# A state-space convolution block: the input's first transform by whole-array matmuls

## The chip, the cores and the metric

The kernel runs on one core of a Trainium2 chip. The metric is the device time of one execution in microseconds (us). A core has a matmul engine (TensorE, PE in the profile), a vector engine (VectorE, DVE), a scalar engine (ScalarE, ACT) that computes functions, a general engine (GpSimd, POOL) and a sync engine (SyncE, SP) that here only issues transfers. TensorE writes to PSUM; VectorE or ScalarE takes the results out ("evacuates" them) to SBUF. Transfers between SBUF and main memory run on 16 DMA engines shared by all queues.

## The reference

The block normalizes its input, runs a long convolution over the sequence, adds the result back through a gate, and then runs a gated feed-forward network. `L` is 2048, `D` is 640. Cut to what matters here:

```python
K = einsum("dn,dnl,dn->dl", Cc, exp(dt*A*l), dt*Bc).real
h = layernorm(x) * (1 + ca) + sa                 # sa, ca, ga, ... = silu(c) @ w_mod
y = irfft(rfft(pad(h)) * rfft(pad(K)))[:L] + h * Dskip
x = x + ga * y
h = layernorm(x) * (1 + cb) + sb
x = x + gb * ((silu(h @ w1) * (h @ w3)) @ w2)
```

The convolution is done per column of `D` over the 2048 positions.

## The kernel before, in words

A position is written as l = 64 a + b, with a below `NA` = 32 and b below `NB` = 64. The transform has two stages: one over a for each b, giving 32 complex frequencies f, and one over b for each f. The host lays the input out with b outermost, so a tile of 128 rows (`ln1_load`, line 366) holds four values of b, each with its 32 values of a. There are 16 such tiles.

The scale (1 + ca) is moved out of the transform into the gate. What is left of the modulation is to add the row r = sa / (1 + ca) to every normalized position. Since the transform is linear, this adds the column sums of the transform's matrix times r. `mod_shift` (line 313) prepares this as `rrow` (r on 64 partitions, line 325) and as `shift` (the product, 320 columns wide with the halves of `D` on the two halves of the partitions, lines 326 to 335).

`u_stage1` (line 389) transforms one tile. For each of its four b it multiplies a 32 by 64 matrix (`s1r`, real and imaginary parts side by side) with 32 rows of the tile, separately for the two halves of `D`: eight matmuls, each on its own 32x64 piece of the array, since the two halves of `D` go to the two halves of the partitions. Two PSUM areas take the results: Z for the first two b, A or B, by the parity of the tile, for the others. In even tiles four matmuls with one row each first put the shift into Z, so that ScalarE can evacuate it with a plain copy (line 409). All other evacuations are VectorE additions of `shift` (lines 411 and 412). Then one transfer stores the tile (line 413) to the scratch `us` in main memory, laid out as half of `D`, part, f, b, columns. A and B are used by the exponentials too (`exp_fast`, `exp_slow`).

`u_load` (line 549) reads it back for the second stage: the convolution's columns are taken in five blocks of 128, and a step fetches eight frequencies of a block to the tile `uk`, with the real part on partitions 0 to 63 and the imaginary part on the others, b within them. It takes two transfers, and four in the third block, which lies across the two halves of `D`. `stage2` (line 559) multiplies input and convolution kernel of a block.

Beside this the kernel makes the convolution kernel: `phases` on GpSimd, sines and exponentials on ScalarE, table products on VectorE (lines 497 to 508), `kgen` and `k_stage1` on TensorE. A first loop over `tk` (10 steps) starts this up. In its first six steps it calls `u_stage1` for two tiles each; tiles 0 to 3 come before it. In it also run `polar` for the remaining columns and `mod_cols`, which multiplies projection weights; the weights are fetched on the same sync queue as the stores and loads of the scratch. At step 7 the loads of the first block are issued. After the loop follow rounds in an order written out by hand (`ROUND`).

ScalarE's instructions stay in the order of the program (`act`, `acopy`). In the loop before the rounds, most instructions of TensorE and VectorE may be reordered by the compiler, which plans with its own cost estimates; at run time each engine's order is fixed.

Of the kernel before, what the change touches and what calls it, by code (L numbers as in the profile page):

```python
# [9 lines left out]
F32 = mybir.dt.float32  # L10
# [3 lines left out]
OP = mybir.AluOpType  # L14
# [3 lines left out]
P = 128  # L18
L = 2048
D = 640  # L20
F = 1728
NA, NB = 32, 64
DC = 128
# [6 lines left out]
KD = D // P  # L30
NFT = 14
WC = 384
# [5 lines left out]
def consts():  # L38

    a = np.arange(NA)[:, None]  # L40
    f1 = np.arange(NA)[None, :]
    ang = 2 * np.pi * a * (f1 + 0.25) / NA
    s1 = np.zeros((4, NA, 2, 4, NA))
    s1r = np.zeros((4, NA, 2, NA))
    for q in range(4):
        s1[q, :, 0, q, :] = np.cos(ang)
        s1[q, :, 1, q, :] = -np.sin(ang)
        s1r[q, :, 0] = np.cos(ang)
        s1r[q, :, 1] = -np.sin(ang)
    s1 = s1.reshape(P, 2, P)  # L50
    s1r = s1r.reshape(P, 2 * NA)
    b = np.arange(NB)[:, None, None]
    g1 = np.arange(NA)[None, :, None]
    f2 = np.arange(NB)[None, None, :]
    th = 2 * np.pi * (b * (g1 + 0.25) / L + b * f2 / NB)
    s2 = np.zeros((2, NB, NA, 2, NB))
    s2[0, :, :, 0] = np.cos(th)
    s2[1, :, :, 0] = np.sin(th)
    s2[0, :, :, 1] = -np.sin(th)
    s2[1, :, :, 1] = np.cos(th)  # L60
    s2 = s2.reshape(P, NA, P)

    i1 = (s2.transpose(2, 1, 0) / L).reshape(2, NB, NA // 2, 2, P).transpose(3, 1, 2, 0, 4).reshape(P, NA // 2, 2, P)
    i2 = np.concatenate([np.cos(ang).T, -np.sin(ang).T] * 2)

    iota = np.zeros((P, NPH), np.int32)
    iota[:, :NA] = -(128 * np.arange(NA) + 63)
    iota[:, NA:] = 2 * np.arange(NA) + 1

    selx = np.tile(np.eye(NA), (4, 1))  # L70
    stepx = np.concatenate([np.arange(NB), 64 * np.arange(NA)])[None].repeat(P, 0)

    c1 = s1r.reshape(4, NA, 2 * NA).sum(axis=1, keepdims=True).repeat(NA, axis=1).reshape(P, 2 * NA)

    one4 = (np.arange(P) % NA == 0).astype(np.float32)[:, None]

    toq = np.arange(P)[:, None] % 4 == np.arange(P)[None] // NA
    tog = np.arange(P)[:, None] // 4 == np.arange(NA)[None]
    misc = np.concatenate([selx, stepx, s1r, c1, one4, toq, tog], axis=1)
# [28 lines left out]
def tile_kernel(ctx: ExitStack, tc: tile.TileContext, a):  # L108
    nc = tc.nc
    V, S, G, PE = nc.vector, nc.scalar, nc.gpsimd, nc.tensor  # L110

    dram = ctx.enter_context(tc.tile_pool(name="dram", bufs=1, space=DRAM))
    us = dram.tile([2, 2, NA, NB, D // 2], F32, name="us")
    zs = dram.tile([NDC, NB, 2, NA, DC], F32, name="zs")
    xs = dram.tile([NT, P, D], F32, name="xs")

# [1 line left out]
    ident = cp.tile([P, P], F32, name="ident")  # L118
# [18 lines left out]
    def acopy(out, in_):  # L137
        return tc.keep_in_program_order(S.copy(out, in_))  # L138
# [15 lines left out]
    s1 = kp.tile([P, 2, P], F32, name="s1")  # L154
# [28 lines left out]
    rrow = pm_.tile([P, D], F32, name="rrow")  # L183
    shift = pm_.tile([P, D // 2], F32, name="shift")
    cols = pm_.tile([P, 7, KD], F32, name="cols")
    lt = pm_.tile([P, 2, D - DC], F32, name="lt")
    misc = pm_.tile([P, 9 * NA + 1 + P], F32, name="misc")
    selx, stepx = misc[:, :NA], misc[:, NA:4 * NA]
    s1r, c1, one4 = misc[:, 4 * NA:6 * NA], misc[:, 6 * NA:8 * NA], misc[:, 8 * NA:8 * NA + 1]
    toq, tog = misc[:, 8 * NA + 1:8 * NA + 1 + P], misc[:, 8 * NA + 1 + P:]  # L190
    tiny = pm_.tile([P, 1], F32, name="tiny")
    V.memset(tiny, -1e-35)

# [119 lines left out]
    def mod_shift():  # L313

        sa, ca, ga, zero, inv, r, gs = (cols[:, i] for i in range(7))
        V.tensor_scalar(ca, ca, 1.0, None, op0=OP.add)
        V.tensor_scalar(zero, ca, 0.0, 1e-18, op0=OP.is_equal, op1=OP.mult)
        V.tensor_tensor(ca, ca, zero, op=OP.add)
        V.reciprocal(inv, ca)
        V.tensor_tensor(r, inv, sa, op=OP.mult)  # L320

        pr = psS.tile([P, 2, 512], F32, name="pr", tag="Z", bufs=1).rearrange("p a b -> p (a b)")
        for k in range(KD):
            PE.matmul(pr[:64, k * P:(k + 1) * P], r[:, k:k + 1].broadcast_to([P, 64]), ident, start=True, stop=True)
        V.tensor_copy(rrow[:64], pr[:64, :D])
        rc = pm_.tile([P, WC], F32, name="part", bufs=2)[:, :KD * 2 * NA].rearrange("p (k c) -> p k c", k=KD)
        V.tensor_tensor(rc, bc(c1, 1, KD), bc(r, 2, 2 * NA), op=OP.mult)
        ps = psS.tile([P, 512], F32, name="ps", tag="pk", bufs=1)
        for k in range(KD):
            for hh in range(2):  # L330
                lo, hi = max(k * P, hh * 320), min(k * P + P, hh * 320 + 320)
                if lo < hi:
                    PE.matmul(ps[hh * 64:hh * 64 + 64, lo - hh * 320:hi - hh * 320], rc[:, k],
                              ident[:, lo - k * P:hi - k * P], start=True, stop=True, tile_position=(0, hh * 64))
        V.tensor_copy(shift, ps[:, :320])

    def mod_gate():

# [24 lines left out]
    hpz = pre.enter_context(tc.tile_pool(name="hpz", bufs=2, side="right"))  # L363
# [19 lines left out]
            x = xt[2 * p + i]  # L383
            act(x, x, AF.Identity, scale=rs[:, 1, i:i + 1], bias=rs[:, 2, i:i + 1])

    usw = us.rearrange("h c f b d -> (h c f) b d")
    usr = us.rearrange("h c f b d -> h c b f d")

    def u_stage1(j):


        x = xt[j]
        u = hpz.tile([P, 4, D // 2], F32, name="u", bufs=2)
        pu = [psS.tile([P, 2, 512], F32, name="pu", tag=t, bufs=1) for t in ("Z", "AB"[j % 2])]
        one = j % 2 == 0
        for q in range(2 if one else 0):
            for hh in range(2):
                PE.matmul(pu[0][hh * 64:hh * 64 + 64, q, :320], c1[q * NA:q * NA + 1],
                          rrow[q * NA:q * NA + 1, hh * 320:hh * 320 + 320],
                          start=True, stop=False, tile_position=(q * NA, hh * 64))  # L400
        for h in range(2):
            for q in range(2):
                r0 = (2 * h + q) * NA
                r = slice(r0, r0 + NA)
                for hh in range(2):
                    PE.matmul(pu[h][hh * 64:hh * 64 + 64, q, :320], s1r[r], x[r, hh * 320:hh * 320 + 320],
                              start=not (one and h == 0), stop=True, tile_position=(r0, hh * 64))
        if one:
            acopy(u[:, :2, :], pu[0][:, :, :320])
        else:  # L410
            V.tensor_tensor(u[:, :2, :], pu[0][:, :, :320], bc(shift, 1, 2), op=OP.add)
        V.tensor_tensor(u[:, 2:, :], pu[1][:, :, :320], bc(shift, 1, 2), op=OP.add)
        nc.sync.dma_start(usw[:, 4 * j:4 * j + 4, :], u)


    ph, cs, AA, EC, PK, K1 = {}, {}, {}, {}, {}, {}
# [132 lines left out]
    def u_load(ch, i):  # L549

        fs = slice(i * 8, i * 8 + 8)
        for h in range(2):
            lo, hi = max(ch * DC, h * 320), min(ch * DC + DC, h * 320 + 320)
            if lo < hi:
                for c in range(2):
                    nc.sync.dma_start(uk[c * 64:c * 64 + 64, 0, fs, lo - ch * DC:hi - ch * DC],
                                      usr[h, c, :, fs, lo - h * 320:hi - h * 320])

    def stage2(ch, g):
        s2 = fp.tile([P, 4, P], F32, name="s2", bufs=3)  # L560
# [207 lines left out]
    rest = polar(d1, G)  # L768
# [5 lines left out]
    for tk in range(LAG):  # L774
# [46 lines left out]
        if tk == 7:  # L821
            for i in range(4):
                u_load(0, i)
# [60 lines left out]
    V, S, G, PE = (InOrder(tc, e, (in_order,)) for e in (V, S, G, PE))  # L884
# [544 lines left out]
```

## Time and profile before

| | us |
|---|---|
| median of 3 runs | 1014.18 |
| lowest and highest run | 1011.33, 1014.97 |
| profiled execution, its span (no other time of it is given) | 1011.9 |
| TensorE busy | 929.3 |
| VectorE busy | 729.6 |
| ScalarE busy | 541.4 |
| GpSimd busy | 347.2 |

The span runs from the first to the last instruction of the profiled execution. Busy time is given in microseconds and, on the page, as share of the span. "PEclk" is TensorE's granted clock, 1.0 being full. "DMA share" is the mean busy share of the 16 DMA engines; above 1 means that packets overlap. In a row of waits stand the waiting engine with tile and line, what it waited for, the total, the number of times and the longest. In rows of operations stand line, engine, operation, output and input tile, count, shortest, median and longest duration in ns, and the starts of the first and the last. In rows of time stand start, duration, engine, line and operation, and in brackets the idle time before it with what ended it. An f32 matmul is two MATMUL instructions, so counts of matmuls are doubled.

### The profile page before, as it was taken

How to read it: one execution, taken by the hardware profiler on the slowest of the kernel's cores; microseconds unless marked ns; L12 is line 12 of the kernel's file. 1: busy time of each engine (PE TensorE's matmuls, PEld its weight loads, DVE VectorE, ACT ScalarE, POOL GpSimd, SP SyncE). 2: the span in 40 equal slices, each digit the busy share in tenths (PEclk: the TensorE clock that was granted, in tenths of full speed). 3: DMA queues.
4: the chain of work that ended last, by engine and by line, in shares of the span. 5: the costliest groups of instructions: out<-in, count | busy, mean ns of one | idle time of the engine just before them, and what ended most of it. 6: DMA issues, size and time to landing. Idle time of an engine off the chain costs nothing.

```text
span 1011.9 us, 20628 instructions
## 1 busy us (share of the span) xinstructions
PE 929.3 (92%) x8214; PEld 691.3 (68%) x8214; DVE 729.6 (72%) x1227; ACT 541.4 (54%) x793; POOL 347.2 (34%) x330
## 2 busy tenths in 40 slices
PE   5898797998998889699999999989979999999998
PEld 2545354666666666467888888766758888888786
DVE  4588856888888885567666676688696666676765
ACT  3667665999999963256433332344643333333432
POOL 1453333444544521123322231453352222224441
PEclk9955777999999999899999999999999999999999
DMA  9463586564556687593211113879332111123352
GB/s 274 140 223 115 204 197 189 142 161 124 138 157 158 176 221 230 171 268 119 80 53 52 52 53 93 218 226 288 98 105 79 53 52 53 52 78 104 92 197 76
DMA packets 103571, 140.74 MB, mean 139 GB/s; under 512 B 20564, under 2 KB 62676, under 8 KB 103476
## 3 DMA queue, kind: packets, MB, share of 16 engines
q1 hardware_dynamic: 92692, 113.60, 39.1%
q10 hardware_dynamic: 8480, 18.09, 6.0%
q0 software_dynamic: 2304, 7.74, 2.3%
q8 instruction: 64, 1.05, 0.4%
q14 instruction: 31, 0.25, 0.1%
HBM read 107.94 MB, written 31.46 MB: 138 GB/s over the span
## 4 chain that ended last, share of the span: by engine, by line
PE 41%; DVE 5%; DMA 3%; issue 2%; ACT 1%; POOL 1%; SPq 1%; DVEq 0%; ACTq 0%; POOLq 0%
PE ps L102 41%; DMA A<-zs 3%; SPq L102 1%; DVE T L102 1%; DVE ul L102 1%; DVE xm L102 1%; DVE gl L102 1%; ACT s L102 1%; DVE s L102 1%; DMA xm<-in_x_dram 1%; ACT gh L102 0%; POOL s L102 0%; POOL S L102 0%; DVE h L102 0%; POOL rs L102 0%
## 5 line engine op out<-in xcount | busy, mean ns | idle before, releaser
L102 DVE TENSOR_TENSOR s<-ps,s 128x512 f32<-128x512 f32 x138 | 94.7, 687 | 76.8 <-PE ps L102 76.3
L472 POOL TENSOR_TENSOR ph<-thi,iota 128x1024 int32<-128x1024 int32 x40 | 85.4, 2135 | 176.1 <-DVE A L508 78.4
L102 DVE TENSOR_TENSOR gl<-rw,gh 128x640 fp32r<-128x640 f32 x87 | 88.1, 1012 | 61.4 <-ACT gh L102 60.1
L102 ACT CAST gh<-rw 128x640 fp32r<-128x640 f32 x87 | 63.2, 726 | 113.5 <-PE ps L102 80.4
L102 POOL TENSOR_TENSOR rw<-rw,gbr 128x512 f32<-128x512 f32 x56 | 81.6, 1465 | 105.4 <-DMA rw<-in_w_dram 91.7
L102 POOL TENSOR_TENSOR S<-rw 128x256 f32<-128x256 f32 x46 | 35.0, 764 | 176.2 <-DVE S0l L102 157.4
L570 PE MATMUL p<-uk,s 128*64 128x256 f32 x640 | 79.1, 390 | 13.3 <-PE pa L432 5.6
L102 PE MATMUL ps<-xA,gh 128*128 128x512 f32 x280 | 88.0, 392 | 1.1 <-DVE h L102 0.4
L102 PE MATMUL ps<-gh,uh 128*128 128x512 f32 x224 | 88.6, 396 | 0.0
L102 PE MATMUL ps<-gl,uh 128*128 128x512 f32 x224 | 88.1, 393 | 0.0
L102 PE MATMUL ps<-gh,ul 128*128 128x512 f32 x208 | 81.9, 394 | 0.0
L570 PEld LDWEIGHTS p<-uk,s 128*64 128x64 f32 x640 | 45.2, 139 | 38.6 <-PE pa L432 8.4
L102 PEld LDWEIGHTS ps<-xA,gh 128*128 128x128 f32 x280 | 52.1, 188 | 14.3 <-ACT gh L102 1.4
L102 PE MATMUL ps<-xA,gl 128*128 128x512 f32 x140 | 54.7, 391 | 1.2 <-DVE gl L102 1.2
L135 ACT ACTIVATE A<-pa 128x1024 f32<-128x1024 f32 x40 | 40.4, 1023 | 26.3 <-PE pa L432 24.9
L497 DVE TENSOR_TENSOR E<-A,cs 128x1024 f32<-128x1024 f32 x40 | 50.1, 1252 | 1.7 <-ACT A L135 1.7
L612 PE MATMUL pz<-Y,i 64*128 64x128 f32 x640 | 45.3, 286 | 5.2 <-ACT zt L138 5.0
L504 DVE TENSOR_TENSOR A<-A,ph 128x1024 f32<-128x1024 f32 x40 | 49.9, 1247 | 0.0
L612 PEld LDWEIGHTS pz<-Y,i 64*128 64x128 f32 x640 | 39.2, 191 | 15.0 <-issue 7.8
L102 PEld LDWEIGHTS ps<-gl,uh 128*128 128x128 f32 x224 | 42.8, 191 | 9.3
L102 PEld LDWEIGHTS ps<-gh,uh 128*128 128x128 f32 x224 | 42.8, 191 | 8.9
L539 PE MATMUL pt<-s,K 128*64 128x128 f32 x640 | 47.3, 291 | 0.5 <-ACT uk L138 0.5
(241 smaller groups left out, 2382.3 us busy)
## 6 DMA issues: line engine op xcount, KB each, us to landing
rw<-in_w_dram ACTq DMA_DIRECT2D x44, 320.0 KB
us<-u SPq DMA_DIRECT2D x16, 640.0 KB
s<-in_s_dram SPq DMA_DIRECT2D x40, 256.0 KB
i<-in_i_dram SPq DMA_DIRECT2D x40, 256.0 KB
rw<-in_wg_dram SPq DMA_DIRECT2D x31, 320.0 KB
rw<-in_wu_dram SPq DMA_DIRECT2D x28, 320.0 KB
uk<-us SPq DMA_DIRECT2D x32, 256.0 KB
zs<-zt SPq DMA_DIRECT2D x32, 256.0 KB
```

Source lines behind the costliest of these rows:

```text
L102: ins = fn(*args, **kw)
L135: return tc.keep_in_program_order(S.activation(*args, **kw))
L472: hold(G.tensor_tensor(p, bc(thi[:, sl], 2, NPH), bc(iota, 1, SD), op=OP.mult))
L497: keep(V.tensor_tensor(EC[s][:, :, 1:3, :], AA[s][:, :, 1:3, :], mid(cs[s]), op=OP.mult))
L504: keep(V.tensor_tensor(A[:, :, 1:3, :], A[:, :, 1:3, :], mid(ph[s]), op=OP.mult))
L539: keep(PE.matmul(pt[c * 64:c * 64 + 64, g, :], kk[:, g, :], s1[:, c, :], start=True, stop=True, tile_position=(0, c * 64)))
L570: keep(PE.matmul(p2[par * 64:par * 64 + 64, pi, c, :], s2[:, pi * 2 + par, c * 64:c * 64 + 64], uk[:, 0:kn + 1:kn, f, :], start=True, stop ...
L612: ins = keep(PE.matmul(pz[:, par, (g % 2) * 2 + pi, :], i1[r, pi, c, :], Y[r, pi, c, :], start=(c == 0), stop=(c == 1), tile_position=(par ...
```

## The change

The transform of a tile uses the matrix `s1`, 128 by 2 by 128, which holds the 32 by 32 matrix four times along its diagonal, once for the real and once for the imaginary part. It was there already, for `k_stage1`. For each of the two parts, two matmuls over all 128 rows and 128 columns, one per half of `D`, fill one PSUM area: Z for the real part, A or B for the imaginary part. Every area is evacuated by VectorE with the shift added; the one-row matmuls and ScalarE's copies are gone. `shift` becomes 2 by 640 columns on all partitions, made by two products in `mod_shift`. The scratch is laid out as part, b, f, columns; the store is still one transfer per tile, and a step of `u_load` is one transfer over 128 partitions.

```diff
-    us = dram.tile([2, 2, NA, NB, D // 2], F32, name="us")
+    us = dram.tile([2, NB, NA, D], F32, name="us")
...
+    c1 = s1.sum(axis=0).T
...
         for k in range(KD):
-            PE.matmul(pr[:64, k * P:(k + 1) * P], r[:, k:k + 1].broadcast_to([P, 64]), ident, start=True, stop=True)
-        V.tensor_copy(rrow[:64], pr[:64, :D])
-        rc = pm_.tile([P, WC], F32, name="part", bufs=2)[:, :KD * 2 * NA].rearrange("p (k c) -> p k c", k=KD)
-        V.tensor_tensor(rc, bc(c1, 1, KD), bc(r, 2, 2 * NA), op=OP.mult)
...
-        V.tensor_copy(shift, ps[:, :320])
+            PE.matmul(pr[:, k * P:(k + 1) * P], r[:, k:k + 1].broadcast_to([P, P]), ident, start=True, stop=True)
+        for c in range(2):
+            V.tensor_scalar(shift[:, c], pr[:, :D], c1[:, c:c + 1], None, op0=OP.mult)
...
-    usw = us.rearrange("h c f b d -> (h c f) b d")
-    usr = us.rearrange("h c f b d -> h c b f d")
+    usw = us.rearrange("c b f d -> (b f) c d")
+    usr = us.rearrange("c b f d -> (c b) f d")
...
         x = xt[j]
-        u = hpz.tile([P, 4, D // 2], F32, name="u", bufs=2)
...
-        if one:
-            acopy(u[:, :2, :], pu[0][:, :, :320])
-        else:
-            V.tensor_tensor(u[:, :2, :], pu[0][:, :, :320], bc(shift, 1, 2), op=OP.add)
-        V.tensor_tensor(u[:, 2:, :], pu[1][:, :, :320], bc(shift, 1, 2), op=OP.add)
-        nc.sync.dma_start(usw[:, 4 * j:4 * j + 4, :], u)
+        u = hpz.tile([P, 2, D], F32, name="u", bufs=2)
+        for c in range(2):
+            pu = psS.tile([P, 2, 512], F32, name="pu", tag="AB"[j % 2] if c else "Z", bufs=1)[:, :, :D // 2]
             for hh in range(2):
+                PE.matmul(pu[:, hh, :], s1[:, c, :], x[:, hh * 320:hh * 320 + 320], start=True, stop=True)
+            V.tensor_tensor(u[:, c].rearrange("p (h d) -> p h d", h=2), pu,
+                            shift[:, c].rearrange("p (h d) -> p h d", h=2), op=OP.add)
+        nc.sync.dma_start(usw[j * P:(j + 1) * P], u)
...
         fs = slice(i * 8, i * 8 + 8)
-        for h in range(2):
...
+        nc.sync.dma_start(uk[:, 0, fs, :], usr[:, fs, ch * DC:ch * DC + DC])
```

More of the change, by code (lines that the diff above doesn't have):

```diff
@@ L43, in consts @@
     s1 = np.zeros((4, NA, 2, 4, NA))
-    s1r = np.zeros((4, NA, 2, NA))
     for q in range(4):
@@ L47, in consts @@
         s1[q, :, 1, q, :] = -np.sin(ang)
-        s1r[q, :, 0] = np.cos(ang)
-        s1r[q, :, 1] = -np.sin(ang)
     s1 = s1.reshape(P, 2, P)
-    s1r = s1r.reshape(P, 2 * NA)
     b = np.arange(NB)[:, None, None]
@@ L71, in consts @@
     stepx = np.concatenate([np.arange(NB), 64 * np.arange(NA)])[None].repeat(P, 0)
-    c1 = s1r.reshape(4, NA, 2 * NA).sum(axis=1, keepdims=True).repeat(NA, axis=1).reshape(P, 2 * NA)
+    c1 = s1.sum(axis=0).T
     one4 = (np.arange(P) % NA == 0).astype(np.float32)[:, None]
@@ L78, in consts @@
     tog = np.arange(P)[:, None] // 4 == np.arange(NA)[None]
-    misc = np.concatenate([selx, stepx, s1r, c1, one4, toq, tog], axis=1)
+    misc = np.concatenate([selx, stepx, c1, one4, toq, tog], axis=1)
     f = lambda v: np.ascontiguousarray(v, dtype=np.float32)
@@ L182, in tile_kernel @@
     scb = pm_.tile([P, KD, NA], F32, name="scb")
-    rrow = pm_.tile([P, D], F32, name="rrow")
-    shift = pm_.tile([P, D // 2], F32, name="shift")
+    shift = pm_.tile([P, 2, D], F32, name="shift")
     cols = pm_.tile([P, 7, KD], F32, name="cols")
     lt = pm_.tile([P, 2, D - DC], F32, name="lt")
-    misc = pm_.tile([P, 9 * NA + 1 + P], F32, name="misc")
+    misc = pm_.tile([P, 5 * NA + 3 + P], F32, name="misc")
     selx, stepx = misc[:, :NA], misc[:, NA:4 * NA]
-    s1r, c1, one4 = misc[:, 4 * NA:6 * NA], misc[:, 6 * NA:8 * NA], misc[:, 8 * NA:8 * NA + 1]
-    toq, tog = misc[:, 8 * NA + 1:8 * NA + 1 + P], misc[:, 8 * NA + 1 + P:]
+    c1, one4 = misc[:, 4 * NA:4 * NA + 2], misc[:, 4 * NA + 2:4 * NA + 3]
+    toq, tog = misc[:, 4 * NA + 3:4 * NA + 3 + P], misc[:, 4 * NA + 3 + P:]
     tiny = pm_.tile([P, 1], F32, name="tiny")
@@ L323, in mod_shift @@
         for k in range(KD):
-            PE.matmul(pr[:64, k * P:(k + 1) * P], r[:, k:k + 1].broadcast_to([P, 64]), ident, start=True, stop=True)
-        V.tensor_copy(rrow[:64], pr[:64, :D])
-        rc = pm_.tile([P, WC], F32, name="part", bufs=2)[:, :KD * 2 * NA].rearrange("p (k c) -> p k c", k=KD)
[L327 to L335, printed above, removed]
+            PE.matmul(pr[:, k * P:(k + 1) * P], r[:, k:k + 1].broadcast_to([P, P]), ident, start=True, stop=True)
+        for c in range(2):
+            V.tensor_scalar(shift[:, c], pr[:, :D], c1[:, c:c + 1], None, op0=OP.mult)
     def mod_gate():
@@ L551, in u_load @@
         fs = slice(i * 8, i * 8 + 8)
[L552 to L557, printed above, removed]
+        nc.sync.dma_start(uk[:, 0, fs, :], usr[:, fs, ch * DC:ch * DC + DC])
     def stage2(ch, g):
```

12 lines of the change are left out of this document (removed).

## The prediction

> **What bounds the kernel now.** I read the page first, then a table of stretches, then the waits and the tile `pu` in the stretches that the change touches.
>
> ```profile
> span 1011.9 us, 20628 instructions
> PEclk9955777999999999899999999999999999999999
> ```
>
> Each figure of the clock row is one fortieth of the span. TensorE has half its clock around 50 to 100 us, part of it to about 175 us, and nearly all of it later. The edited code runs in that slow part. The stretches, with busy time per engine, granted clock and DMA share:
>
> ```profile
> 38.00:52.00 14.00, 11.71 (x85) 5.39 (x78) 6.33 (x16) 12.12 (x14) 9.54 (x9) 0.91 0.20 71
> 52.00:118.00 66.00, 57.97 (x696) 31.17 (x697) 56.80 (x106) 46.02 (x56) 24.87 (x24) 0.58 0.49 175
> 118.00:136.00 18.00, 14.31 (x124) 6.91 (x120) 12.36 (x19) 10.02 (x11) 8.87 (x7) 0.58 0.50 188
> 136.00:170.00 34.00, 28.77 (x405) 17.41 (x402) 20.54 (x32) 20.30 (x25) 10.95 (x6) 0.77 0.76 185
> 170.00:340.00 170.00, 154.09 (x2983) 113.10 (x2978) 147.57 (x241) 156.90 (x192) 75.31 (x47) 1.00 0.57 154
> ```
>
> Columns after the length are PE, weight loads, DVE, ACT, POOL, clock, DMA share, GB/s. From 170 us the hand-ordered rounds run against ScalarE (156.90 of 170), so what ends before 170 moves everything behind it one for one. Between 52 and 118 VectorE (56.80 of 66) and TensorE at 0.58 clock (57.97) share the bound; ScalarE has 20 us to spare. The chain of waits on the page reaches back only to 453 us, so the early part must be argued from waits:
>
> ```profile
> ACT u L138 <- PE pu L406: 9.3, 2, 7.6
> PE pu L406 <- ACT u L138: 6.2, 3, 3.6
> DVE u L412 <- PE pu L406: 5.0, 2, 4.8
> DVE u L411 <- PE pu L406: 3.3, 4, 2.0
> ```
>
> The transform and its evacuations already hold each other up: TensorE waited 6.2 us for ScalarE's copies, VectorE 8.3 us (5.0 + 3.3) for TensorE.
>
> **The change part by part.** What the transform takes now (operation rows, then the same tile by stretch):
>
> ```profile
> L406 PE MATMUL pu<-x,misc x256: 426/737/792, 41.9 to 128.2; 32*64 32x320 f32 x128
> L398 PE MATMUL pu<-rrow,misc x64: 427/736/792, 38.6 to 118.8; 1*64 1x320 f32 x64
> L412 DVE TENSOR_TENSOR u<-pu,shift x16: 805/818/826, 44.4 to 127.1; 128x640 f32<-128x640 f32 x16
> L138 ACT COPY u<-pu x8: 670/690/693, 48.7 to 126.5; 128x640 f32<-128x640 f32 x8
> ...
> 38.00:52.00 14.00, 5.64 (x36) 1.71 (x36) 0.82 (x1) 0.67 (x1) 0.91 0.20 71
> 52.00:118.00 66.00, 30.73 (x244) 9.86 (x244) 15.36 (x19) 4.11 (x6) 0.58 0.49 175
> 118.00:136.00 18.00, 4.56 (x40) 1.28 (x40) 3.24 (x4) 0.69 (x1) 0.58 0.50 188
> ...
> sum 132.00, PE 40.92 PEld 12.85 DVE 19.43 ACT 5.47; mean PE 10.23 PEld 3.21 DVE 4.86 ACT 1.37
> ```
>
> *Evacuations.* Eight copies leave ScalarE (5.47 us), eight additions of 0.82 us come to VectorE. Six of the copies lie in 52 to 118 (x6), where VectorE is idle for only 9.2 us, mostly waiting in order at its head: 6 x 0.82 = 4.9 us on the path. The bounds are 0 (all in the idle time) and 6.6 (all eight). I take 4.9. ScalarE's 5.47 us are worth nothing themselves, since it has slack; but TensorE's 6.2 us of waiting for those copies, which sat in ScalarE's written order, become waits for VectorE. I credit -2, between 0 and -6.2.
>
> *Matmuls.* Each tile of 128 rows now needs 8 matmuls on 32x64 pieces, plus 4 one-row ones for even tiles; afterwards 4 on the whole array, one behind the other. An f32 matmul shows as two passes. Prices:
>
> ```profile
> 76.86 1.35 PE L406 MATMUL pu<-x,misc 32*64 32x320 f32 x8
> 115.67 0.80 PE L406 MATMUL pu<-x,misc 32*64 32x320 f32 x16 [1.87 <-ACT u L138]
> ...
> 165.13 1.22 PE L357 MATMUL pm<-part,misc 128*128 128x256 f32 x2 [0.25 <-DVE modT L353]
> ```
>
> At half clock four pieces together took 1.35 us, at full clock eight took 0.80. As pieces run side by side, each group is two passes of 320 columns and a tail; equal tails give 2 x (1.35 - 0.80) = 1.10 us of streaming at half clock and 0.55 at full. The whole-array row agrees: 1.22 us for 256 columns at half clock is 0.88 of streaming by the same rate, and a tail of 0.34. So 16 x 4 = 64 matmuls cost 35 us at full clock and 70 at half, against 40.92 now: -6 to +29 us of TensorE time.
>
> The Trainium skill, "TensorEngine Tiling (Array Packing)", Overview and Key Properties, speaks against the edit: pieces of the array run independently, up to 16 at once. By that rule alone the old form would be 24 rounds (16 tiles and 8 one-row rounds), 26 us at half clock, and the edit would cost 44 us, an estimate. The trace bears the side-by-side running out, but not the 26 us: the old form takes 40.92, since its groups lie scattered between other shapes.
>
> Which clock? Three pieces of the slow part:
>
> ```profile
> 49.35:97.10 47.75, 45.88 (x454) 24.92 (x454) 40.01 (x72) 32.33 (x41) 20.70 (x20) 0.50 0.47 166
> 93.72:97.13 3.41, 3.41 (x80) 2.96 (x68) 2.55 (x4) 3.36 (x6) 1.59 (x2) 0.50 0.29 86
> 63.00:66.41 3.41, 3.41 (x46) 1.52 (x34) 2.13 (x6) 2.46 (x3) 1.23 (x2) 0.50 0.96 345
> 97.10:100.50 3.40, 0.15 (x2) 0.00 (x0) 3.15 (x8) 3.39 (x4) 2.35 (x2) 1.00 0.57 154
> ```
>
> TensorE shows busy 45.88 of 47.75 us and stays at 0.50. The full stretch 63.00 to 66.41, mostly 32-row pieces, did not raise the clock; the equally full 93.72 to 97.13, with 128-row operands of `kgen` and `k_stage1`, did. Then 3.4 us almost without matmuls lost it again. The new matmuls have 128 rows, so I expect rises, and losses when an evacuation keeps them waiting: about 0.75 on average. Then the 64 cost 47 us (70 x 0.5 / 0.75), 6 more than now; other TensorE work in 52 to 118, 57.97 - 30.73 = 27.2 us, falls to 21 (27.2 x 0.58 / 0.75), 6 less. Net 0 there. The Trainium skill, "TensorE: Matmul & The Clock Gate", Part 1, gives full clock after one busy window of about 3.4 us; 63.00 to 66.41 disagrees unless few rows count as idle, and 93.72 to 97.13 agrees.
>
> *Waits of VectorE.* Its 24 additions waited 8.3 us for TensorE, 0.35 each; 8 more make +2.8. Behind each stand the table products that `kgen` waits for. Bounds 0 and, at half clock where a pair of matmuls takes 2.2 us instead of 1.35, 32 x 0.85 = 27. I take 2.8, the present rate.
>
> *The first and last tiles.* Tiles 0 and 1 come at a clock of 0.91, where VectorE idles anyway:
>
> ```profile
> 44.38 0.82 DVE L412 TENSOR_TENSOR u<-pu,shift 128x640 f32<-128x640 f32 x1 [4.85 <-PE pu L406]
> 42.45 2.39 PE L406 MATMUL pu<-x,misc 32*64 32x320 f32 x18
> 41.86 0.79 PE L398 MATMUL pu<-rrow,misc 1*64 1x320 f32 x1
> ```
>
> They run from 41.86 to 44.84, 3.0 us; eight matmuls at 0.55 and a tail make 4.7: +1.7, all on the path, since the next projection matmuls queue behind. Tiles 14 and 15 (4.56 us in the 118 stretch) would take 4.7 to 9.1, with the following matmuls at the better clock: I take +1, bounds -2 and +4.5.
>
> *The shift rows.*
>
> ```profile
> 33.85 0.47 DVE L327 TENSOR_TENSOR part<-misc,cols 128x320 f32<-128x320 f32 x1
> 35.77 1.76 PE L333 MATMUL ps<-ident,part 128*64 128x128 f32 x12
> 36.02 0.82 DVE L325 COPY rrow<-pr 64x640 f32<-64x640 f32 x1 [1.05 <-PE pr L324]
> 37.57 0.49 DVE L335 COPY shift<-ps 128x320 f32<-128x320 f32 x1 [0.74 <-PE ps L333]
> ```
>
> Gone: 1.76 of TensorE and 0.47 + 0.82 + 0.49 = 1.78 of VectorE. Come: two products of 640 columns, 0.82 each by L325's row, 1.64. Bank Z is held through both, to about 37.7 instead of 36.8. I take -0.5, bounds -1.8 and +0.9.
>
> *Scratch.* Stores keep number and bytes; a partition writes two pieces instead of one. Per load step of `u_load` one DMA replaces two (four for the third channel block).
>
> ```profile
> 134.49 2.87 SPq L556 DMA_DIRECT2D uk<-us  x4
> 145.24 3.69 SPq L556 DMA_DIRECT2D uk<-us  x4
> ...
> 138.00:142.00 4.00, 0.56 1.23 199
> 4.00:5.00 1.00, 1.00 1.09 285
> ...
> 144.00:146.00 2.00, 1.00 0.30 22
> ```
>
> (After the length stand clock, DMA share and GB/s.) The sync queue issues 8 loads in 6.6 us before the rounds; four save about 3, but behind them the first `s2` loads meet busy DMA engines. The loads moved 199 GB/s with all engines busy; the parameters' 512-byte pieces, whose rows lie 2560 bytes apart, moved at 285 (4 to 5 us). The new scratch has such rows too: 2.1 MB at 285 instead of 199 is 7.4 instead of 10.5 us. No row shows the new address order, so the bounds are -3.1 and +3.1; I take -1, because the DMA engines were nearly empty from 144 to 146, so not all of a gain there reaches `p`. In the rounds (DMA share 0.57) nothing comes of it; were that cover gone, the four later blocks would bring four times that.
>
> Sum: 4.9 - 2 + 0 + 2.8 + 1.7 + 1 - 0.5 - 1 = +6.9 us on 1011.9, 1018.8 us. The median of the runs, 1014.18, is 2.3 above the profiled span; with it 1021.1.
>
> **Rivals.**
> *Half clock stays (B).* If evacuations break up the matmuls, the 64 cost 70 us, +29. TensorE is idle for 98 - 83.99 = 14.0 us between 38 and 136 (the table's three stretches); used up wholly that leaves +15, not at all +29: 1029 to 1043. For: 0.50 for 47 us of full queues. Against: 128-row work raised the clock.
>
> *The clock is released (C), the faster side.* It decides from a mean clock of about 0.9 between 49 and 136. The 64 cost 39 us, and waits for TensorE go: VectorE's 8.3, TensorE's 6.2 for ScalarE, and half of the first of these two of ScalarE's:
>
> ```profile
> 136.13 1.08 ACT L135 ACTIVATE A<-pq 128x512 f32<-128x512 f32 x2 [4.69 <-PE pq L444]
> 169.51 0.59 ACT L138 COPY kc<-p 128x512 f32<-128x512 f32 x1 [8.65 <-PE p L570]
> ```
>
> That is up to 8.3 + 6.2 + 2.3 (half of 4.69) = 16.8 less, against 4.9 + 1.7 + 1 = 7.6 more: -9, 1005. Against: VectorE's 56.80 us grow to 61.7, so there is little room; and bank Z alternates between TensorE and VectorE. By the Trainium skill, "TensorE: Matmul & The Clock Gate", Part 1, this is the case that would follow.
>
> *Nothing reaches the end (D).* VectorE's 9.2 idle us take the six additions, and ScalarE's 8.65 us wait at 169.51 absorbs the rest: 1014. Against: `p` there is itself late with the transforms.
>
> **How the numbers follow.** Chances: the sum (A) 0.52, B 0.15, C 0.15, D 0.18. A's own range is 1014 to 1029. For 8 in 10 the range runs from 1008 (most of D, a part of C) to 1035 (the lower half of B). A change of 0.5%, 5 us, is about what can be told from none here. Four fifths of A and all of B are slower by more: 0.57. D and the rest of A: 0.28. C: 0.15.
>
> **What would show it.** The stretch from the first `u` product to the last store (44 to 130 us) lengthens by 5 to 8 us, VectorE's busy time there grows by some 6.6, and ScalarE's first `kc`, now 169.51, comes as much later. Clock between 49 and 97 above 0.50 shows the 128-row reading right; `pu` near 70 us of TensorE shows B. The first `u_load`s at over 199 GB/s show the row order counts. Wrong I would be if the compiler's order of the unpinned instructions shifts more than the edit itself: VectorE's order between 44 and 136 is its choice.

## The result, and the profile after

Over 18 runs of each, the changed kernel took 1011.35 us in the median (1005.42 to 1016.36) and the kernel before 1013.21 (1007.56 to 1015.93): a ratio of 0.9991, 95% interval 0.9974 to 1.0008. That is no change; I had forecast 0.7% slower. Run beside other kernels later, the changed kernel gave 1.0000 (0.9976 to 1.0024). The profiled execution of the changed kernel took 1011.42 us, its span 1009.6.

Span and clock row of its page, and the same stretches as in the prediction (busy time of PE, weight loads, DVE, ACT, POOL, then clock, DMA share, GB/s):

```profile
span 1009.6 us, 20187 instructions
...
PEclk9987989999999999999999999999999999999999
```

```profile
38.00:52.00 14.00, 11.95 (x76) 7.73 (x76) 8.53 (x16) 8.19 (x10) 6.21 (x6) 0.88 0.40 140
52.00:118.00 66.00, 49.21 (x452) 32.33 (x450) 58.38 (x105) 44.52 (x53) 26.01 (x25) 0.84 0.45 150
118.00:136.00 18.00, 12.50 (x111) 7.21 (x111) 16.58 (x26) 7.49 (x8) 9.20 (x7) 0.81 0.45 165
136.00:170.00 34.00, 28.59 (x454) 18.88 (x455) 21.06 (x34) 21.55 (x25) 12.36 (x8) 0.90 0.74 216
170.00:340.00 170.00, 154.05 (x2984) 113.11 (x2982) 147.07 (x240) 156.90 (x192) 74.78 (x47) 1.00 0.52 154
```

The clock, 0.58 before in 52 to 118 and in 118 to 136, is now 0.84 and 0.81. VectorE is busier by 2.20, 1.58 and 4.22 us in the first three stretches, 8.0 us in all. The new tile `pu`, its stretch and its sum from 38 to 136, and what waited around it between 36 and 136:

```profile
52.00:118.00 66.00, 30.63 (x86) 18.04 (x86) 16.21 (x21) 0.84 0.45 150
...
sum 98.00, PE 47.39 PEld 27.34 DVE 25.28; mean PE 15.80 PEld 9.12 DVE 8.43
```

```profile
PE pu L382 <- ACT x L131: 9.9, 4, 4.6
DVE u L383 <- PE pu L382: 9.2, 6, 2.9
...
PE pu L382 <- DVE u L383: 4.4, 4, 2.0
```

TensorE spends 47.39 us on the transforms (40.92 before), VectorE 25.28 us on the additions (19.43), and VectorE still waits 9.2 us for TensorE. The last store of the scratch is issued at 135.5 us instead of 129.9. So the last store comes 5.6 us later, where the sum up to there had 7.9. But ScalarE's first `kc`, which was to come as much later, moved by half a microsecond (169.51 before):

```profile
170.01 0.59 ACT L134 COPY kc<-p 128x512 f32<-128x512 f32 x1 [5.49 <-PE p L537]
```

Where the delay was made good shows between the front and the first product `p` of the rounds. I take as the front the first ten projection matmuls behind the last transform. First the kernel before, then the changed one: the front, the start of the next group of projection matmuls, the first `p`, and the stretches directly behind the front.

```profile
130.26 2.79 PE L299 MATMUL pm<-uk,scb 128*32 128x384 f32 x10
...
140.29 1.42 PE L299 MATMUL pm<-uk,scb 128*32 128x384 f32 x4
...
166.28 3.18 PE L570 MATMUL p<-uk,s 128*64 128x256 f32 x16
```

```profile
130.00:135.00 5.00, 5.00 (x32) 2.57 (x31) 1.06 (x2) 1.44 (x2) 2.95 (x2) 0.50 0.43 144
135.00:141.00 6.00, 6.00 (x69) 4.09 (x69) 3.95 (x7) 2.28 (x4) 0.00 (x0) 0.50 1.14 267
```

```profile
134.63 1.48 PE L294 MATMUL pm<-uk,scb 128*32 128x384 f32 x10
...
141.28 0.83 PE L294 MATMUL pm<-uk,scb 128*32 128x384 f32 x2
...
166.34 3.62 PE L537 MATMUL p<-uk,s 128*64 128x256 f32 x16
```

```profile
134.00:139.00 5.00, 4.79 (x91) 2.65 (x90) 2.17 (x5) 0.95 (x2) 2.94 (x2) 1.00 0.87 297
139.00:142.00 3.00, 3.00 (x38) 1.95 (x34) 2.93 (x5) 2.28 (x5) 0.00 (x0) 1.00 1.11 344
```

Before, TensorE was busy for all of the 11 us from 130 to 141, at half clock: the ten matmuls took 2.79 us, and the next group started 10.0 us after them. After, the ten matmuls run at full clock, in 1.48 us, and the next group starts after 6.65 us. The fronts lie 4.4 us apart; from front to `p` it is 36.0 us before and 31.7 after, so 4.3 of the 4.4 are won back there. The compiler has also put other instructions between these rows than before, so the rows alone do not say that the clock did it; the experiments come back to this.

### The profile page after: what moved, and what is told of

The parts are those of the page before. It is cut to its first block, busy times and chain, and to the rows that moved or that the text cites. A ratio compares the mean times of both kernels' runs of the same rounds, so it can differ in the third digit from the quotient of the medians.

```text
span 1009.6 us, 20187 instructions
## 1 busy us (share of the span) xinstructions
PE 916.0 (91%) x8010; PEld 694.8 (69%) x8010; DVE 735.1 (73%) x1234; ACT 536.6 (53%) x785; POOL 349.5 (35%) x330
## 4 chain that ended last, share of the span: by engine, by line
PE 60%; ACT 14%; DVE 11%; DMA 6%; issue 5%; POOL 3%; SPq 0%; ACTq 0%; DVEq 0%; POOLq 0%
PE ps L98 45%; ACT cs L131 3%; DMA A<-zs 3%; ACT A L131 3%; PE p L537 3%; ACT ph L131 2%; PE pq L416 2%; PE pu L382 2%; PE pa L404 2%; ACT L131 2%; DMA zs<-zt 1%; PE pk L493 1%; PE pz L579 1%; DMA rw<-in_w_dram 1%; PE pt L511 1%
## 5 line engine op out<-in xcount | busy, mean ns | idle before, releaser
L382 PE MATMUL pu<-x,s 128*128 128x320 f32 x128 | 47.4, 520 | 17.7 <-ACT x L131 9.9
L382 PEld LDWEIGHTS pu<-x,s 128*128 128x128 f32 x128 | 27.3, 227 | 34.3 <-ACT x L131 11.4
```

Source lines behind the costliest of these rows:

```text
L382: PE.matmul(pu[:, hh, :], s1[:, c, :], x[:, hh * 320:hh * 320 + 320], start=True, stop=True)
```

## Experiments

Three theories stood against each other. T1: the additions cost about 4.9 us on VectorE's path, and the released clock paid them back. T2: they cost as much, but the faster scratch loads paid. T3: nothing in this stage reaches the end; the projection matmuls set its time anyway. All ratios are to the kernel before, run beside. The table at the end of this section has front, first product and first `kc` of every run.

**One: the old pieces and scratch, every evacuation on VectorE** (`e1`), so that the one-row matmuls go too.

```diff
-        one = j % 2 == 0
+        one = False
```

> The old pieces and the old scratch, with all evacuations on VectorE and no one-row matmuls. Theory 1 (the additions cost VectorE 4.9 us on the path, and in the changed kernel the released clock paid that back): the clock between 52 and 118 us stays near 0.58, and the time is 3 to 7 us above the kernel before. Theory 2 (the additions cost that much, and faster scratch loads paid it back): the same 3 to 7 us here. Theory 3 (nothing of this stage reaches the end, since the projection matmuls before the first stage-2 product set its time): within 1.5 us of the kernel before, with ScalarE's first copy of a stage-2 result within 1 us of 169.5.

1014.26 us, ratio 1.0039 (1.0018 to 1.0061): about 4 us slower. Stretch 52 to 118, then front, next group and first product:

```profile
52.00:118.00 66.00, 47.08 (x556) 25.81 (x556) 60.33 (x108) 44.92 (x53) 26.87 (x25) 0.61 0.44 159
```

```profile
133.83 2.77 PE L299 MATMUL pm<-uk,scb 128*32 128x384 f32 x10 [1.25 <-DVE u L411]
...
143.69 0.83 PE L299 MATMUL pm<-uk,scb 128*32 128x384 f32 x2
...
168.78 3.12 PE L570 MATMUL p<-uk,s 128*64 128x256 f32 x16
```

The time grows by about what the additions were priced at; the clock stays at 0.61 and the ten matmuls at 2.77 us. T3 does not fit. The compiler orders unpinned instructions anew for each kernel, so this is not the additions quite alone. Between front and `p` it gave `e1` the order of the changed kernel: VectorE's instructions stand there in the same order, TensorE's nearly so. So `e1` has the changed kernel's order with the old half clock, and there the next group starts 9.9 us behind the front, against 6.65.

**Two and three: the old pieces with the scratch in the order half, part, b, f**, with the old evacuations (`e2`) and with all on VectorE (`e3`).

```diff
-        nc.sync.dma_start(usw[:, 4 * j:4 * j + 4, :], u)
+        for h in range(2):
+            for c in range(2):
+                nc.sync.dma_start(usw[h, c, :, 4 * j:4 * j + 4, :],
+                                  u[h * 64 + c * 32:h * 64 + c * 32 + 32])
```

> The old pieces and evacuations, with the scratch in the order half, part, b, f (the store of a tile in four transfers of 32 partitions). Theory 2: the scratch loads run at 285 GB/s or more instead of 199, and the time falls by 3 us or more. Theories 1 and 3: the loads may be as fast, and the time stays within 1.5 us of the kernel before.

> Both of these together, so that only the whole-array matmuls are missing against the changed kernel. Theory 1: no release of the clock, 3 to 7 us above the kernel before. Theory 2: within 2 us of the kernel before, as the changed kernel is. Theory 3: within 1.5 us.

1059.36 us, ratio 1.0491 (1.0471 to 1.0510), and 1048.91 us, 1.0385 (1.0366 to 1.0403). Both miss every expectation. The stores of `e2`, and its longest waits of ScalarE in 38 to 175:

```profile
L414 SPq DMA_DIRECT2D us<-u x64: 302/438/1939, 48.1 to 173.5; - x64
```

```profile
ACT u L138 <- PE pu L405: 33.4, 5, 14.8
...
ACT x L135 <- DVE rs L381: 18.7, 1, 18.7
```

A tile now leaves in four stores of 32 partitions, 64 in all, and the last comes at 173.5 us. ScalarE stands 33.4 us in front of copies whose matmuls are not done, and 18.7 us for one normalization. Store form and instruction order changed together, so the times of these two runs say nothing on the order of addresses. They do show that what is late at the front is late at the end: in `e2` the first `kc` comes at 215.8 us, 46.3 later than in the first profile of the kernel before, and the time is 4.9% longer.

**Four: the changed kernel with half of its real parts copied by ScalarE** (`e4`), which leaves the shift out of these parts.

```diff
+            if c == 0 and j % 2 == 0:
+                acopy(u[:, c].rearrange("p (h d) -> p h d", h=2), pu)
+                continue
             V.tensor_tensor(u[:, c]...
```

> The changed kernel with the real part of the even tiles copied out by ScalarE again; the shift is left out of these eight evacuations. Theories 1 and 2: VectorE's eight additions are worth 3 to 6 us, so the time is 3 to 6 us below the changed kernel, 4 to 7 below the kernel before. Theory 3, or VectorE's idle time taking the additions: within 1.5 us of the changed kernel.

1010.83 us, ratio 1.0001 (0.9977 to 1.0026): no gain from 6.5 us less on VectorE, where T1 and T2 had 3 to 6 us; T3 had it. Front, next group, a later group that waits for its weights, first product:

```profile
131.46 1.48 PE L294 MATMUL pm<-uk,scb 128*32 128x384 f32 x10
...
137.04 0.84 PE L294 MATMUL pm<-uk,scb 128*32 128x384 f32 x4
...
150.60 0.96 PE L294 MATMUL pm<-uk,scb 128*32 128x384 f32 x2 [3.50 <-DMA uk<-in_w_mod_dram]
...
165.42 3.29 PE L540 MATMUL p<-uk,s 128*64 128x256 f32 x16
```

The front came at 131.5 us, but a later group of projection matmuls then stood 3.5 us for the transfer of its weights. From front to `p` it is 34.0 us: what VectorE gave was lost to the next thing that was late. Here VectorE's instructions between front and `p` stand in the order of the kernel before, and TensorE's nearly so, but at full clock: the next group starts 5.6 us behind the front, where the kernel before needs 10.0.

**Five and six: what makes the scratch loads fast.** `e5` puts the rows of the new scratch 40,960 bytes apart instead of 2,560, with every engine's order unchanged; `e6` cuts every load into two transfers of 64 partitions.

```diff
-    us = dram.tile([2, NB, NA, D], F32, name="us")
+    us = dram.tile([2, NB, NA, 16 * D], F32, name="us")[:, :, :, :D]      # e5
...
-        nc.sync.dma_start(uk[:, 0, fs, :], usr[:, fs, ch * DC:ch * DC + DC])
+        for r in (slice(0, 64), slice(64, P)): nc.sync.dma_start(uk[r, 0, fs, :], usr[r, fs, ch * DC:ch * DC + DC])      # e6
```

> The changed kernel with its scratch rows 40,960 bytes apart instead of 2,560; the instructions of every engine stand in the same order. T2 (the faster scratch loads paid the additions back): the first loads fall from some 290 GB/s back towards 199, the first kc comes 3 to 6 us later and the time is 3 to 6 us above the changed kernel's, a ratio of 1.002 to 1.005 to the kernel before. T1 (the released clock paid) and T3 (nothing of this stage reaches the end before the projection matmuls do): the loads slow down and the time stays, 0.999 with 0.003 either way.

> The changed kernel with every step of scratch loads as two transfers of 64 partitions, as before, instead of one of 128; address order as in the change. If the number of partitions of a transfer made the loads faster, their packets go back towards 50 ns and 199 GB/s; if the nearness of the pieces did, they stay near 34 ns and 290 GB/s. For the time: T2 with the first cause 1.002 to 1.005; otherwise all theories 0.999 with 0.003 either way, as only the issues on SP double.

1010.82 us, 0.9997 (0.9976 to 1.0018), and 1013.11 us, 1.0023 (0.9995 to 1.0050). The stretch 142 to 145, filled by these loads, in the changed kernel, in `e5` and in `e6` (last columns clock, DMA share, GB/s), and then front and product of `e6`:

```profile
142.00:145.00 3.00, 2.48 (x27) 1.19 (x28) 1.59 (x3) 2.46 (x4) 1.82 (x1) 1.00 1.17 288
```

```profile
142.00:145.00 3.00, 2.48 (x30) 1.40 (x26) 0.96 (x2) 2.51 (x4) 2.38 (x2) 1.00 1.20 291
```

```profile
142.00:145.00 3.00, 2.67 (x26) 0.98 (x26) 2.23 (x3) 2.45 (x4) 1.19 (x1) 1.00 1.23 199
```

```profile
135.26 1.48 PE L294 MATMUL pm<-uk,scb 128*32 128x384 f32 x10
...
166.97 3.62 PE L537 MATMUL p<-uk,s 128*64 128x256 f32 x16
```

Far rows load as fast as near ones (291 and 288 GB/s). Halving the partitions brings back the 199 GB/s of before. Over all the loads ahead of the rounds the mean 512-byte packet took 33.0 ns in the changed kernel, 32.9 in `e5`, 49.4 in `e6` and 48.4 before; `e2`, with b ahead of f in the scratch as in the change but 64 partitions in a transfer, has 50.2. All theories had expected slow loads in `e5`; as they stayed fast, only `e6` tests T2. The Trainium skill, "DMA: Bandwidth & Descriptors", Rules for kernel authors, advises one transfer over 128 partitions rather than two over disjoint halves, since both halves use the same 16 engines; the 199 against 288 agree with the advice. That the engines are shared does not say why two halves are slower; this stays open. The ratio of `e6` lies in the 1.002 to 1.005 that T2 gave, but its interval reaches from no loss to all of that, so it does not decide. The profile does: with slow loads `e6` still goes from front to `p` in 31.7 us, as the changed kernel does in its first profile. So the loads did not win back the time between front and `p`, and T2 falls there.

**Seven: all real parts on ScalarE** (`e9`), the shift added to `pu` by a one-row matmul over the whole array.

```diff
+                if c == 0:
+                    PE.matmul(pu[:, hh, :], c1r[:1], shift[:1, 0, hh * 320:hh * 320 + 320], start=False, stop=True)
+            if c == 0:
+                acopy(u[:, c].rearrange("p (h d) -> p h d", h=2), pu)
+                continue
```

> The changed kernel with the real part of all 16 tiles copied by ScalarE and its shift added by a one-row matmul on the whole array: VectorE gives up 16 additions of some 0.82 us (13 us), TensorE gets 32 matmuls of 0.55 us, ScalarE 16 copies. T1 (VectorE's busy time in this stage counts, the clock paid it back): 5 to 8 us below the changed kernel, ratio 0.991 to 0.994. T3 (the end of the stage is set by the projection matmuls and the leg behind them, not by VectorE's additions): 0.997 to 1.001, as with half as many copies.

1038.32 us, ratio 1.0279 (1.0238 to 1.0320), a miss for both. ScalarE's longest wait from 36 to 165:

```profile
ACT u L135 <- PE pu L386: 49.3, 11, 8.6
```

ScalarE keeps the program's order, so each copy holds up the sines and exponentials behind it: 49.3 us in 11 waits. The front came at 159.6 us.

**Eight: the first experiment with the clock pushed up** by two whole-array matmuls per tile whose result is overwritten (`e10`).

```diff
+        for hh in range(2):
+            PE.matmul(pu[1][:, hh, :320], s1[:, 0, :], x[:, hh * 320:hh * 320 + 320], start=True, stop=True)
```

> The kernel before, all evacuations on VectorE, in its old pieces and old scratch order (as in the first experiment, 1.0039), with two whole-array matmuls per tile more, whose result the next one overwrites. T1: the 128-row operands raise the granted clock in 52 to 118 from 0.61 to over 0.75, the projection matmuls after 118 run at full clock and most of the 4 us comes back, ratio 0.999 to 1.001, although TensorE does 32 matmuls more (18 us at full clock). T2: the loads stay at some 199 GB/s, so the ratio stays at 1.003 to 1.006. T3: the clock rises and the ratio falls back to 0.999 to 1.001 only if the projection matmuls end earlier.

1019.37 us, ratio 1.0068 (1.0036 to 1.0099), a miss for T1.

```profile
52.00:118.00 66.00, 54.59 (x604) 29.28 (x603) 57.86 (x106) 43.13 (x51) 23.36 (x23) 0.77 0.50 173
```

The clock rose to 0.77, yet TensorE's busy time grew from 47.08 to 54.59 us. At the front the ten matmuls still took 2.77 us; the clock rose behind them (0.85 in the 11 us from the front on), and from front to `p` it is 34.3 us, 0.6 less than in `e1`. In the time nothing came back: here a clock bought with extra work did not pay.

**Nine and ten: the changed kernel with the transform in pieces of 32 by 32**, written with four row groups side by side (`e11`), and with the two loops exchanged, so that the halves of one row group come behind each other (`e12`).

```diff
-                PE.matmul(pu[:, hh, :], s1[:, c, :], x[:, hh * 320:hh * 320 + 320], start=True, stop=True)
+                for r in [slice(q * NA, q * NA + NA) for q in range(4)]: PE.matmul(pu[r, hh, :], s1[r, c, r], x[r, hh * 320:hh * 320 + 320], start=True, stop=True, tile_position=(r.start, r.start))
```

> The changed kernel with its new scratch order and all its additions on VectorE, but the first transform again in pieces of 32 rows, now by 32 columns, four side by side. Against the first experiment (1.0039) it differs by the 128-partition loads, against the changed kernel by the pieces. T1 (the clock paid back): the granted clock in 52 to 118 falls from 0.84 to about 0.6, the projection matmuls after 134 take 2.8 us again, and the ratio is 1.003 to 1.005. T2 (the loads paid back): it stays where the changed kernel is, 0.998 to 1.001. Half and half: 1.001 to 1.003, the first kc between 170 and 172.

> The run with 32 by 32 pieces, with the two halves of the columns of one row group behind each other, so that two row groups overlap instead of four. If the number of row groups fed at a time sets the clock: the granted clock in 52 to 118 falls from 0.84 towards the 0.6 of the kernel before, the first ten projection matmuls take 2.8 us, the first product comes 35 us after them, ratio 1.004 to 1.008. If it does not: clock 0.8 to 0.85, 1.5 us, 30 us, ratio 1.001 to 1.004.

1015.44 us, 1.0028 (1.0009 to 1.0047), and 1015.92 us, 1.0039 (1.0015 to 1.0064). Stretch 52 to 118 of `e11`, its front and product, the stretch of `e12`, and 16 pieces of each, `e11` first:

```profile
52.00:118.00 66.00, 50.12 (x732) 25.55 (x732) 59.27 (x105) 44.99 (x53) 25.68 (x25) 0.84 0.45 155
```

```profile
135.53 1.48 PE L294 MATMUL pm<-uk,scb 128*32 128x384 f32 x10 [0.30 <-DVE u L383]
...
165.84 2.81 PE L537 MATMUL p<-uk,s 128*64 128x256 f32 x16
```

```profile
52.00:118.00 66.00, 52.01 (x716) 27.99 (x718) 57.83 (x101) 42.46 (x51) 27.42 (x26) 0.84 0.48 165
```

```profile
67.61 1.28 PE L382 MATMUL pu<-x,s 32*32 32x320 f32 x16
```

```profile
69.25 1.30 PE L382 MATMUL pu<-x,s 32*32 32x320 f32 x16 [0.36 <-DVE u L383]
```

With 32-row pieces the clock is the same 0.84, and front to `p` takes 30.3 and 31.5 us: T1's forecast for `e11`, a clock of about 0.6, is a miss. So the higher clock does not need 128-row operands. Whether the number of row groups side by side matters is not shown: in the trace the pieces of `e12` start in fours within 0.1 us, as those of `e11` do, and 16 of them take 1.30 and 1.28 us, so nothing says that fewer ran at a time. The ratios of both lie 0.3 to 0.4% above the changed kernel's. `e11` has its first `kc` at 168.7, no later than the changed kernel, so its difference does not show in this stage; `e12` has it at 173.1.

**Eleven: 8 additions more in the changed kernel** (`e8`).

> The changed kernel with 8 additions more on VectorE (the real part of the even tiles is added twice into the same place), 8 x 0.82 = 6.5 us. T1: VectorE's time counts one for one in this stage, the last scratch store moves from 135.5 to about 142 and the first kc from 170 to about 176, ratio 1.005 to 1.007. T3: the 27.5 us in which VectorE stands idle between 38 and 170 take them and the ratio stays at 0.998 to 1.001.

1021.02 us, ratio 1.0097 (1.0068 to 1.0126); the changed kernel beside it 1010.71, 10.3 us less for 6.5 us of additions.

```profile
180.62 0.59 ACT L134 COPY kc<-p 128x512 f32<-128x512 f32 x1 [2.55 <-PE p L540]
```

The front came at 148.5 us and `kc` at 180.6. VectorE's work does reach the end (0.97% with an interval of 0.3 either way), and T3 falls. The size is not that of the additions alone, since the compiler's order of TensorE and VectorE changed with them; T1 had 0.5 to 0.7%.

**Repeats.** The changed kernel beside the last two (`c0`); then three more profiles of the kernel before and one more of the changed one (`c1` to `c4`).

> The changed kernel once more, beside the others of this call, so that they can be set against it on the same chip. All theories: 0.999 with 0.002 either way, the first kc at 170 and the last scratch store at 135.5, each within 1 us.

> The kernel before once more. If the changed kernel pays its additions back by the released clock: the projection matmuls after the last scratch store start near 130 us, take 2.8 us for their first ten, and the first product (p) comes about 36 us after them, against 30 to 32 us in the changed kernel. If the first comparison was chance: start and distance scatter by 4 us and overlap with those of the changed kernel.

> As the run beside it: start near 130 us, distance to the first product 36 us within 1 us if the clock pays; overlap with the changed kernel's 134 to 139 and 30 to 32 us if it was chance.

> As the two runs beside it: start near 130 us, distance to the first product 36 us within 1 us if the clock pays; overlap with the changed kernel's 134 to 139 and 30 to 32 us if it was chance.

> The changed kernel once more: start of the projection matmuls at 134 to 139 us, their first ten in 1.5 us, the first product 30 to 32 us after them if the clock pays; a distance of 33 us and more if it was chance.

`c0`: 1010.71 us, ratio 1.0000 (0.9976 to 1.0024), but its last store came at 139.9 and its `kc` at 172.5, 4.4 and 2.5 us off the first profile, a miss of the 1 us expected (the execution profiled was its slowest, 1019.11 us). The other four are single runs: 1012.21, 1015.55, 1014.80 and 1013.31 us, with one more run of the kernel before at 1007.75. Front and product of `c1`, then of `c0`:

```profile
128.44 2.79 PE L299 MATMUL pm<-uk,scb 128*32 128x384 f32 x10
...
164.45 3.14 PE L570 MATMUL p<-uk,s 128*64 128x256 f32 x16
```

```profile
138.67 1.48 PE L294 MATMUL pm<-uk,scb 128*32 128x384 f32 x10
...
169.25 3.18 PE L537 MATMUL p<-uk,s 128*64 128x256 f32 x16
```

All runs, in us (front: first ten projection matmuls behind the last transform; ten: their time):

```
run                    front    ten   first p   front to p   first kc   ratio
before                130.26   2.79    166.28      36.0       169.51
c1 (before)           128.44   2.79    164.45      36.0       167.64
c2 (before)           127.84   2.79    164.25      36.4       167.53
c3 (before)           128.49   2.79    164.91      36.4       168.19
changed               134.63   1.48    166.34      31.7       170.01    0.9991
c0 (changed)          138.67   1.48    169.25      30.6       172.48    1.0000
c4 (changed)          138.28   1.48    168.87      30.6       172.10
e5 far rows           133.99   1.48    164.17      30.2       166.17    0.9997
e6 two loads          135.26   1.48    166.97      31.7       170.65    1.0023
e4 half on ScalarE    131.46   1.48    165.42      34.0       168.76    1.0001
e11 32x32 pieces      135.53   1.48    165.84      30.3       168.68    1.0028
e12 32x32, pairs      138.15   1.48    169.62      31.5       173.11    1.0039
e8 8 more additions   148.49   1.48    178.62      30.1       180.62    1.0097
e9 all on ScalarE     159.60   1.48    191.04      31.4       193.04    1.0279
e1 old, all VectorE   133.83   2.77    168.78      35.0       171.93    1.0039
e10 the same, warmed  135.35   2.77    169.66      34.3       173.20    1.0068
e3 old, all, rows     166.86   2.77    203.00      36.1       205.00    1.0385
e2 old, rows          173.09   2.77    212.66      39.6       215.82    1.0491
```

Four profiles of the kernel before have the front at 128.8 on average. Four of the changed program (the first, `c0`, `c4`, and `e5`, whose instructions stand in the same order) have it at 136.4: 7.6 later, and not overlapping. From front to product they take 36.2 and 30.8 us: 5.4 less, again without overlap. The clock in 52 to 118 is 0.58 to 0.60 in the four of the kernel before, and 0.79 to 0.84 in those of the changed program.

How much of the 5.4 us is the clock, and how much the new order? `e1` has the changed order at the old clock: 35.0 us, 4.2 above the 30.8 of the changed program (3.2 to 4.8 above the four) and 1.2 below the 36.2 of the kernel before. `e4` has the old order at full clock: the gap to the next group falls from between 9.3 and 10.0 us to 5.6, and front to `p` to 34.0, with 3.5 us of waiting for weights in it. So by these two runs, each profiled once, the clock gave some 4 us of the 5.4 and the order about 1. T1 holds in this form: additions and transforms put the front 7.6 us later, and 5.4 came back between front and first product, most of it by the clock.

## Why the prediction was wrong

*The front.* The terms up to the last store came to 7.9 us; the four profiles of each show 7.6 at the front and 9.1 at the last store (128.4 and 137.5 on the mean). The additions' 4.9 us stand beside 5 us at the front and about 4 us in the time of the first experiment. But the total is right in part by luck, since several terms are not. TensorE's transform time of 47 us was 47.39, though at a clock of 0.84 in place of 0.75 the same price gives 42 (70 x 0.5 / 0.84). Its other work in 52 to 118 fell to 18.6 us (49.21 - 30.63), where 21 was expected; but only 366 other instructions lie in the stretch (452 less 86), where there were 452 (696 less 244), so a part of it is work that moved. VectorE's waits for TensorE grew from 8.3 to 9.2 us in the first profile, where 2.8 more were expected. The credit of 2 us for TensorE's waits came in its own terms: 6.2 us for ScalarE's copies became 4.4 for VectorE. But its waits for the normalized tiles, which the sum did not have, grew to 9.9 us (both rows stand in the result); before they were

```profile
PE pu L406 <- ACT x L135: 3.1, 1, 3.1
```

so TensorE's waits of these two kinds grew from 9.3 to 14.3 us.

*The step that failed* is the last term of the tiles: tiles 14 and 15 "with the following matmuls at the better clock: I take +1, bounds -2 and +4.5". The better clock was applied in full to the stretch of the transforms; what follows them was in this term, which came out as a loss and allowed a gain of 2 us at most. The rows for it were there: 0.77 in 136 to 170, and in finer stretches 11 us at 0.50 with TensorE wholly busy. With the change the next group of projection matmuls comes 6.65 us behind the front instead of 9.3 to 10.0, and until `p` the gain is 5.4 us, some 4 of it by the clock (`e1`) and about 1 by the compiler's new order, for which the sum had no term. 7.6 - 5.4 leaves 2.2 us for the first product, and the means of `kc` (168.2 and 170.2) differ by 2.0.

*One for one.* What ends before 170 did move the rest: `kc` later by 47.6, 36.8, 24.8 and 12.4 us than the mean of before goes with 50, 39, 28 and 10 us in the time (`e2`, `e3`, `e9`, `e8`; their ratios times 1012). For the 2.0 us of the changed kernel this can't be tested: its median stands at 0.9 us below the kernel before, interval 2.6 below to 0.8 above. From `kc` to the end of the span the four profiles of before take 842.4 to 845.5 us and those of the changed program 839.4 to 844.8, so whether 2 us came back there too stays open.

*The loads.* The rate of 285 GB/s was right (288), the reason was not: one transfer over all partitions in place of two over halves set it (199 in `e6`), not the distance of the rows (291 in `e5`). So the right rate was luck. And the gain of 1 us to `p` is not seen: `e6`, at the old rate, takes the same 31.7 us.

*The clock.* That it would rise was right; that it takes 128-row operands fell with `e11`. They may still raise it: in `e10`, two whole-array products per tile more went with 0.77 in place of 0.61. What keeps it low beside pieces of 32 by 64 (0.58 and 0.61) and not beside 32 by 32 (0.84) is not settled. The Trainium skill, "TensorE: Matmul & The Clock Gate", Part 1, gives full clock after one busy window of about 3.4 us. The kernel before, which the trace shows busy from 130 to 141 at 0.50, disagrees.

*The rivals.* D named the time that came (1014), but not the way: VectorE's idle time did not take the additions, as the front and `e8` show. C's mechanism was at work, in another place: VectorE's waits for TensorE did not go (9.2 us), the matmuls behind the transforms gained. In B's terms the transforms would have shown near 70 us; they show 47.39.

## What to carry over

When a change moves a clock or a rate, apply it to everything on that engine until the next stage begins, and price the stretch directly behind the edit in fine windows, where a fully busy engine at half clock stands out. Where the compiler orders instructions anew, look for runs that have one order at both clocks, as `e1` and the changed kernel have here, before the clock gets all of a gain. Before reading a few microseconds out of two profiles, take each kernel's profile again: here the same program put its front at 134 and at 139. And for pieces as short as these, a load that covers all 128 partitions in one transfer is to be preferred to two halves (288 against 199 GB/s), but count it as a gain only where its consumer waits for it.

## What was not expected of the hardware

- Loads of 512-byte pieces: 288 GB/s and 33 ns a packet over 128 partitions, 199 GB/s and 49 ns as two transfers over 64 (`e6`); rows 40,960 bytes apart cost nothing (291 GB/s, `e5`).
- TensorE busy for 11 us without a gap at a granted clock of 0.50 (130 to 141 in the kernel before), and 0.84 in 52 to 118 with 32 by 32 pieces as with whole-array matmuls.
- Eight additions of 0.82 us, 6.5 us in all, made the time 10.3 us longer (`e8`, where the compiler's order changed too) in a stage in which VectorE showed 27.5 us idle between 38 and 170 (132 less 104.55, from the four stretches above).
